# Pooled attention with a gated feed-forward block: order of the first loads and the copies of batch 0

## Chip, core and metric

One core of a Trainium2 chip. Times are device microseconds (us) of one execution. Its engines are TensorE (PE, with its weight loads as PEld), VectorE (DVE), ScalarE (ACT), GpSimd (POOL) and SyncE (SP); each works through its own queue in order.

## What is computed

q, k and v have 8 batches, 8 heads, 576 positions and 64 elements. k and v are averaged over groups of 8 positions, so that 72 keys and values remain; each of the 576 queries attends to these. The result goes, as 4608 tokens of 512 elements, through two matrices with a gate between them:

```
k_p = k.reshape(B, H, Sp, pool, D).mean(axis=3)
v_p = v.reshape(B, H, Sp, pool, D).mean(axis=3)
attn = softmax(scale * q @ k_p^T)
x = (attn @ v_p), heads side by side
h = x @ w_in
out = (h * cos(h)) @ w_out
```

## The kernel before

There are nine token tiles of 512 and eight batches of 576. The order of the work on each engine is the order in which it is written. Attention of batch 0 comes first, by itself; then, for each tile t, the up-projection (`up_mm`, L297, with cos on ScalarE L304 and the product on VectorE L307) and the down-projection (`down_mm`, L310), with the attention of the next batch filled in between the matmuls of the down-projection. Batches from 2 on are pooled by POOL (`pool_add`) and turned by DMA transposes; batches 0 and 1 are pooled and turned on TensorE.

**Layout of batches 0 and 1.** A tile of k, q or v has 128 partitions: the even head of a pair in partitions 0 to 63, the odd head in 64 to 127, nine positions in each partition, four pairs side by side. Pooling is a matmul with a matrix `groups` of ones and zeros, which VectorE builds from two iotas of POOL through `dist`, `sign` and `groups` (L361 to L365).

**PSUM.** `banks[0..2]` are three pairs of banks, `obanks[0]` and `obanks[1]` two single ones.

**The loads.** k's first two pairs come as fp32 by SP (L342) into a part of `g_sb` that is free then, and ScalarE casts them into the k tile (L343). All others are issued by POOL, with the cast in the transfer (L84): behind the three iotas (L347, L350) q's first two pairs, k's last two, q's last two, v, and then weights and batch 1.

**Batch 0, in the order written** (L397 to L420):
1. Ten warm-up matmuls; pooling of k's pairs 0 and 1 (`pool_k_mm`, 36 matmuls of 64x72, L157, even and odd heads in two halves of the partitions of obank1); four copies into `kk` by VectorE (`put_kk`, L132): each half is put on both halves of the partitions of `kk`.
2. Two warm-ups; nine transposes of q (`q_transpose_mm`, L192): blocks 0 to 4 into bank2, copied by VectorE, 5 to 8 into obank0, copied by ScalarE (L193). Two warm-ups.
3. Scores (L211) and exp (L218) of the first two units. A unit is 256 queries of four heads; `us[0]` and `us[1]` are heads 0 to 3, `us[2]` and `us[3]` are heads 4 to 7.
4. Pooling of k's pairs 2 and 3 into obank1, its four copies, the sums of `us[0]` (`sums_first`: matmuls with ones L266, then 1/sum on ScalarE as ln and exp, L270 and L271), transposes 9 to 17 of q into bank2 and obank0 and two copies, the sums of `us[1]` (obank1).
5. Scores and exp of `us[2]` and `us[3]` (`banks[0]` and `banks[2]`); pooling of v (`pool_v_mm`, L165, 18 matmuls 256 wide into the two banks of `banks[1]`) and one copy (L167); the sums of `us[2]` and `us[3]` and the values of all four (`values_then`: matmuls L280, product on VectorE L282 into `xT`).
6. The first quarter of the up-projection needs heads 0 to 3 alone (`up_mm(0, 0, 0, 2)`, `up_mm(0, 1, 0, 2)`), the rest all heads.

**Batch 1.** During tile 0, beside the up-projection (fp 4 to 6), k is pooled (pairs 0 and 1 into obank0, copied by VectorE, pairs 2 and 3 into obank1, copied by ScalarE) and q is transposed; v is pooled in the down-projection (L468).

Of the kernel before, what the change touches and what calls it, by code (L numbers as in the profile page):

```python
# [19 lines left out]
def kernel(  # L20
# [9 lines left out]
    nc = tc.nc  # L30
    B, H, S, D = q.shape
    Sp = S // POOL
# [4 lines left out]
    KCH = d_model // 128  # L37
# [9 lines left out]
    REST = (SEG[2], (0, H))  # L47
# [19 lines left out]
    kk = [wpool.tile([128, H, SpA], BF16, name=f"kk{i}") for i in range(2)]  # L67
# [4 lines left out]
    banks = [psum.tile([128, 2, 512], FP32, name=f"bank{i}") for i in range(3)]  # L72
# [5 lines left out]
    staged = {}  # L78
# [4 lines left out]
    def load_even(dst, b, src, j0=0, j1=KCH):  # L83
        nc.gpsimd.dma_start(out=dst[:, j0:j1].rearrange("p j t d -> p j (t d)"), in_=even_view(src, b, j0, j1))  # L84
# [38 lines left out]
    half = (slice(0, 64), slice(64, 128))  # L123

    def v_part(b):
        return vz[b % 2][:, :, 0:4:3, :]

    def put_kk(b, ps, pj0, pj1, copy):
        dst = kk[b % 2].rearrange("p (j a) n -> p j a n", a=2)
        for a in range(2):  # L130
            for r in range(2):
                copy(out=dst[half[r], pj0:pj1, a, 0:Sp], in_=ps[half[a]])  # L132

    def pool_add(b, which):

        st = staged.pop((which, b))
# [10 lines left out]
            s = s.rearrange("p (j a) t d -> p j a t d", a=2)  # L147
            add(out=v_part(b), in0=s[..., 0, :], in1=s[..., 1, :], op=ADD)

    def pool_k_mm(b, bank, pj0, pj1):  # L150

        kb = staged["k", b]
        ps = bank[:, 0:(pj1 - pj0) * Sp].rearrange("p (j n) -> p j n", n=Sp)
        for pj in range(pj0, pj1):
            for t in range(ROW):
                for rows in half:
                    nc.tensor.matmul(ps[rows, pj - pj0, :], lhsT=kb[rows, pj, t, :], rhs=groups[rows, t, :],  # L157
                                     start=(t == 0), stop=(t == ROW - 1))
        return lambda copy: put_kk(b, ps, pj0, pj1, copy)

    def pool_v_mm(b, pair):
        vb = staged["v", b]
        for t in range(ROW):
            for hp, rows in enumerate(half):
                nc.tensor.matmul(pair[:Sp, hp, 0:KCH * D], lhsT=groups[rows, t, :], rhs=vb[rows, :, t, :],  # L165
                                 start=(t == 0), stop=(t == ROW - 1))
        nc.vector.tensor_copy(out=v_part(b).rearrange("p j a d -> p a j d"),  # L167
                              in_=pair[:Sp, :, 0:KCH * D].rearrange("p a (j d) -> p a j d", j=KCH))

    def k_transpose(b):  # L170
        nc.sync.dma_start_transpose(out=kk[b % 2], in_=kp2[b % 2].rearrange("p h s d -> p (h s d)"))
# [14 lines left out]
    def q_transpose_mm(b, bank, g0, g1):  # L186

        if ("qT", b) not in att:
            qT_tile(b)
        ps = bank.bitcast(BF16)[:, 0:(g1 - g0) * 128].rearrange("p (g n) -> p g n", n=128)  # L190
        for g in range(g0, g1):
            nc.tensor.matmul(ps[:, g - g0, :], q_flat(b)[:, g * 128:(g + 1) * 128], identity, is_transpose=True)  # L192
        return lambda copy: copy(out=att["qT", b][:, g0:g1, :], in_=ps)  # L193
# [80 lines left out]
    def values_then(b, u, ao):  # L274

        (c0, n), (h0, nh) = u
        ex = att.pop(("ex", b, u))
        for i in range(nh):
            pj, hp = divmod(h0 + i, 2)
            nc.tensor.matmul(ao[hp * 64:hp * 64 + 64, (i // 2) * n:(i // 2 + 1) * n],  # L280
                             lhsT=vz[b % 2][:, pj, 3 * hp, :], rhs=ex[:, ex_col(u, i):ex_col(u, i) + n])
        nc.vector.tensor_mul(out=x_out(b, u, slice(0, 128)), in0=cols(ao, u), in1=cols(att.pop(("inv", b, u)), u))  # L282
# [58 lines left out]
    k_first = g_sb.rearrange("p f n -> p (f n)").bitcast(FP32)[:, 0:2 * ROW * D]  # L341
    nc.sync.dma_start(out=k_first.rearrange("p (j n) -> p j n", j=2), in_=even_view(k, 0, 0, 2))  # L342
    nc.scalar.copy(out=staged["k", 0][:, 0:2].rearrange("p j t d -> p (j t d)"), in_=k_first)  # L343

    row_of = consts.tile([128, ROW], FP32, name="row_of")
    for rows in half:
# [2 lines left out]
    first_of = consts.tile([128, Sp], FP32, name="first_of")  # L349
    nc.gpsimd.iota(first_of, pattern=[[POOL, Sp]], base=0, channel_multiplier=0,  # L350
                   allow_small_or_imprecise_dtypes=True)
    load_even(staged["q", 0], 0, q, 0, 2)
    load_even(staged["k", 0], 0, k, 2, 4)
    load_even(staged["q", 0], 0, q, 2, 4)
    load_even(staged["v", 0], 0, v)
# [33 lines left out]
    def warm_up(n, bank):  # L389

        for i in range(n):
            nc.tensor.matmul(bank, lhsT=warm[:, 0:128], rhs=warm)
# [2 lines left out]
    us = BY_HEADS  # L395

    warm_up(10, obanks[0])  # L397
    pool_k_mm(0, obanks[1], 0, 2)(vec)
    warm_up(2, banks[1][:, 0, :])
    puts = q_transpose_mm(0, banks[2][:, 0, :], 0, 5), q_transpose_mm(0, obanks[0], 5, 9)  # L400
    puts[0](vec)
    puts[1](act)
    warm_up(2, banks[1][:, 0, :])
    scores(0, us[0], banks[0])
    scores(0, us[1], banks[1])
    pool_k_mm(0, obanks[1], 2, 4)(vec)
    sums_first(0, us[0], banks[0][:, 0, :])
    for put in (q_transpose_mm(0, banks[2][:, 0, :], 9, 14), q_transpose_mm(0, obanks[0], 14, 18)):
        put(vec)
    sums_first(0, us[1], obanks[1])  # L410
    warm_up(2, banks[1][:, 0, :])
    scores(0, us[2], banks[0])
    scores(0, us[3], banks[2])
    pool_v_mm(0, banks[1])
    sums_first(0, us[2], obanks[0])
    values_then(0, us[0], obanks[1])
    values_then(0, us[1], banks[1][:, 0, :])
    sums_first(0, us[3], banks[2][:, 0, :])
    values_then(0, us[2], obanks[1])
    values_then(0, us[3], obanks[0])  # L420
# [4 lines left out]
    for t in range(NT):  # L425
        b = t + 1
        if t > 0:

            up_mm(t, 0, 0, 2)
            up_mm(t, 1, 0, 2)  # L430
        for fp in range(FFCH // 2):
            up_mm(t, fp, 2 if fp < 2 else 0)
            between = ()
            if t == 0:
                if fp == 4:
                    puts = pool_k_mm(1, obanks[0], 0, 2), pool_k_mm(1, obanks[1], 2, 4)
                elif fp in (5, 6):
                    g0 = 9 * (fp - 5)
                    puts = q_transpose_mm(1, obanks[0], g0, g0 + 5), q_transpose_mm(1, obanks[1], g0 + 5, g0 + 9)
                if fp in (4, 5, 6):  # L440
                    puts[0](vec)
                    between = ((puts[1], act),)
            up_g(t, fp, between)
            if 0 < t and b < B:
                if fp == 0:
                    q_transpose(b)
                elif fp == 2:
                    k_transpose(b)
        mms = [(ms, fc) for ms in range(4) for fc in range(FFCH)]
        if t == 0:  # L450
            mms = [(ms, fc) for hm in range(2) for cg in range(4) for ms in range(2 * hm, 2 * hm + 2)
                   for fc in range(4 * cg, 4 * cg + 4)]


        def S_(n, bank):
            return lambda: scores(b, us[n], banks[bank])

        later = []

        def V_(n, bank, wait=None):  # L460
            return lambda: values(b, us[n], banks[bank], wait)

        fill = []
        if t < B:
            exp_tables()
            fill = [(1, lambda: scores(t, REST, banks[2])), (16, lambda: values(t, REST, banks[1]))]
        if t == 0:
            fill[1:] = [(2, S_(0, 0)), (8, lambda: pool_v_mm(1, banks[1])), (8, lambda: values(t, REST, banks[2])),  # L468
                        (11, S_(1, 0)), (13, V_(0, 1)), (18, S_(2, 2)), (21, V_(1, 0, later)), (26, S_(3, 1)),
                        (32, lambda: later.pop()()), (32, V_(2, 2)), (40, V_(3, 0))]  # L470
        elif b < B:
            us = BY_TOKENS

            def scores_of(*parts):

                def go():
                    for f in scores_mm, scores_exp:
                        for b_, u, bank in parts:
                            f(b_, u, banks[bank])
                return go  # L480

            fill = [(4, scores_of((b, us[0], 2), (b, us[1], 0))), (14, V_(0, 1, later)), (16, lambda: later.pop()()),
                    (19, V_(1, 2)), (35, scores_of((b, us[2], 0), (b, us[3], 1), (t, REST, 2))),
                    (38, V_(2, 0)), (43, lambda: values(t, REST, banks[1])), (46, V_(3, 2))]
        fi = 0
        if t == NT - 1:
            mms = mms[:-FFCH]
        for n, (ms, fc) in enumerate(mms):
            while fi < len(fill) and fill[fi][0] <= n:
                fill[fi][1]()  # L490
                fi += 1
            down_mm(obanks[ms % 2], ms, fc)
            if fc == FFCH - 1:
                down_out(t, ms, obanks[ms % 2])
        if t < B:
            sin_tables()
        if 0 < t and b + 1 < B:

            nc.gpsimd.tensor_copy(out=gate, in_=kk[b % 2][0:1, 0, 0:1])  # L499
        if b + 1 < B:  # L500
            load_kv(b + 1, "k", k)
            load_q(b + 1)
            load_kv(b + 1, "v", v)
            pool_add(b + 1, "k")
            pool_add(b + 1, "v")
# [29 lines left out]
```

The softmax here doesn't subtract the row's maximum and nothing guards it: scores larger than these inputs give would overflow.

## Time and profile before

| what | us |
|---|---|
| median of four runs | 302.15 (301.62 to 302.44) |
| the profiled execution | 301.98 |
| its span | 300.2 |
| TensorE busy | 291.5 |
| ScalarE busy | 205.6 |
| VectorE busy | 171.0 |
| POOL busy | 130.5 |

By the chain that ended last, TensorE carries 91% of the span. Times of rows count from the start of the span. A row of the timeline has a start, the busy time, the engine, line, operation, what it writes and reads, its shape and number, and in brackets the idle time before it with what ended it. The granted clock of TensorE is given as 1.00 for the core. From about 4 us to 33 us the DMA engines carry 190 to 210 GB/s.

### The profile page before, as it was taken

To read this page: it belongs to the slowest core of one execution; us is meant where nothing else is said; L and a number is where in the kernel's file an instruction comes from. 1 tells how busy PE (TensorE), PEld (TensorE's weight loads), DVE (VectorE), ACT (ScalarE), POOL (GpSimd) and SP (SyncE) were. 2 spreads that over 40 slices of the span, in tenths; PEclk is the share of its full clock that TensorE was granted. 3 is DMA by queue.
4 is the path that set the end of the run, shared out by engine and by line. 5 is a ranking of instruction groups with operands and counts; after the bars stand their busy time and mean duration, and the time that the engine had idled before them with its cause. 6 is when DMAs were issued, how large, how long until landed. Compare 5 with 4: busy or idle time off the path is not lost.

```text
span 300.2 us, 4592 instructions
## 1 busy us (share of the span) xinstructions
PE 291.5 (97%) x1783; PEld 143.2 (48%) x1816; DVE 171.0 (57%) x212; ACT 205.6 (68%) x254; POOL 130.5 (43%) x93
## 2 busy tenths in 40 slices
PE   8899999999999999999999999999999999999995
PEld 3545544445544454445444544455445544444444
DVE  5558546574566546754675566654675477415712
ACT  3887896469866987688768886789568966605500
POOL 8463018975963497339813990399200000000000
PEclk9999999999999999999999999999999999999999
DMA  7999999739436942696079617791811120131023
GB/s 159 202 207 207 209 203 194 161 57 177 91 81 120 174 106 49 133 169 129 17 156 153 133 23 171 102 168 37 142 31 35 37 70 0 37 70 35 0 67 75
DMA packets 44165, 32.91 MB, mean 110 GB/s; under 512 B 22128, under 2 KB 39408, under 8 KB 44144
## 3 DMA queue, kind: packets, MB, share of 16 engines
q0 software_dynamic: 19744, 18.07, 38.3%
q1 hardware_dynamic: 24160, 14.42, 20.5%
q8 instruction: 14, 0.23, 0.3%
q10 hardware_dynamic: 240, 0.13, 0.2%
q14 instruction: 7, 0.06, 0.1%
HBM read 36.70 MB, written 9.44 MB: 154 GB/s over the span
## 4 chain that ended last, share of the span: by engine, by line
PE 91%; ACT 2%; issue 1%; DVE 0%
PE bank L297 41%; PE obank L310 40%; PE bank L241 5%; PE bank L211 3%; PE bank L328 1%; ACT ex L218 1%; PE obank L157 0%; ACT inv L271 0%; PE bank L165 0%; ACT lnc L270 0%; PE obank L192 0%; DVE xT L282 0%; DVE o_sb L316 0%
## 5 line engine op out<-in xcount | busy, mean ns | idle before, releaser
L310 PE MATMUL obank<-w_out_sb,g_sb 128*128 128x512 bf16 x542 | 129.0, 379 | 0.9 <-issue 0.2
L297 PE MATMUL bank<-xT,w_in_sb 128*128 128x512 bf16 x563 | 126.0, 379 | 0.8
L304 ACT ACTIVATE cos<-bank,half_pi 128x1024 f32<-128x1024 f32 x72 | 79.3, 1113 | 58.9 <-PE bank L297 57.7
L307 DVE TENSOR_TENSOR g_sb<-bank,cos 128x1024 bf16<-128x1024 f32 x72 | 87.4, 1224 | 42.5 <-ACT cos L304 42.4
L297 PEld LDWEIGHTS <-w_in_sb 128*128 128x128 bf16 x576 | 56.1, 98 | 67.9 <-issue 1.9
L310 PEld LDWEIGHTS <-g_sb 128*128 128x128 bf16 x560 | 52.7, 98 | 56.6 <-issue 2.0
L252 DVE TENSOR_TENSOR xT<-bank,inv 64x512 bf16<-64x512 f32 (+1 forms) x72 | 45.3, 629 | 40.8 <-ACT inv L248 40.1
L141 POOL TENSOR_TENSOR kv_st<-kv_st 72x2048 f32<-72x2048 bf16 x12 | 48.7, 4060 | 33.2 <-DMA kv_st<-in_k_dram 33.2
L247 ACT ACTIVATE lnc<-bank 64x512 f32<-64x512 f32 (+1 forms) x72 | 39.2, 544 | 3.1 <-PE bank L241 1.7
L316 DVE COPY o_sb<-obank 128x512 f32<-128x512 f32 x35 | 23.6, 690 | 30.9 <-PE obank L310 30.5
L218 ACT ACTIVATE ex<-bank 72x1024 bf16<-72x1024 f32 (+1 forms) x40 | 35.0, 929 | 8.5 <-PE bank L211 8.4
L142 POOL TENSOR_TENSOR kv_st<-kv_st 72x1024 f32<-72x1024 f32 x12 | 28.2, 2347 | 1.0
L248 ACT ACTIVATE inv<-lnc 128x512 f32<-128x512 f32 (+1 forms) x36 | 21.0, 583 | 1.1
L241 PE MATMUL bank<-ex,vz 72*128 72x256 bf16 (+1 forms) x176 | 20.0, 243 | 0.1
L241 PEld LDWEIGHTS <-vz 72*128 72x128 bf16 x176 | 13.6, 97 | 9.6 <-DVE xT L252 0.5
L145 POOL TENSOR_TENSOR kp<-kv_st 72x512 bf16<-72x512 f32 x12 | 14.9, 1265 | 0.5
L211 PE MATMUL bank<-qT,kk 64*72 64x256 bf16 (+1 forms) x192 | 12.9, 251 | 0.5 <-issue 0.3
L499 POOL COPY gate<-kk 1x1 bf16<-1x1 bf16 x5 | 0.9, 182 | 26.5 <-DMA kk<-kp 26.5
L211 PEld LDWEIGHTS <-kk 64*72 64x72 bf16 x192 | 7.5, 109 | 9.9 <-issue 7.2
L285 ACT ACT_TABLE_LOAD x9 | 11.5, 1283 | 0.9 <-PEq L519 0.7
L288 ACT ACT_TABLE_LOAD x9 | 11.5, 1283 | 0.2
L103 POOL DMA_DIRECT2D kv_st<-in_v_dram x6 | 5.1, 848 | 8.8 <-PE bank L165 8.8
(55 smaller groups left out, 93.3 us busy)
## 6 DMA issues: line engine op xcount, KB each, us to landing
out_dram<-o_sb SPq DMA_DIRECT2D x70, 128.0 KB, 2.4
kv_st<-in_v_dram POOLq DMA_DIRECT2D x8, 576.0 KB, 13.6
kv_st<-in_k_dram POOLq DMA_DIRECT2D x7, 576.0 KB, 7.5
q_b<-in_q_dram POOLq DMA_DIRECT2D x6, 576.0 KB, 9.7
w_in_sb<-in_moe_w_in_dram POOLq DMA_DIRECT2D x4, 512.0 KB, 13.2
w_out_sb<-in_moe_w_out_dram POOLq DMA_DIRECT2D x4, 512.0 KB, 18.5
q_b<-in_q_dram POOLq DMA_DIRECT2D x4, 288.0 KB, 11.9
g_sb<-in_k_dram SPq DMA_DIRECT2D x1, 576.0 KB, 3.7
```

Source lines behind the costliest of these rows:

```text
L141: add(out=s, in0=x[:, :, 0:4, :], in1=x[:, :, 4:8, :], op=ADD)
L142: add(out=s[:, :, 0:2, :], in0=s[:, :, 0:2, :], in1=s[:, :, 2:4, :], op=ADD)
L211: nc.tensor.matmul(pair[:Sp, bank, c:c + n].rearrange("p (g n) -> p g n", n=64), lhsT=kk[b % 2][half[r], h0 + i, 0:Sp], rhs=att["qT", b][h ...
L218: nc.scalar.activation(out=ex[:, 0:nh * n].rearrange("p (a n) -> p a n", a=2), in_=pair[:Sp, :, 0:nh * n // 2], func=ACTF.Exp, scale=scale ...
L241: nc.tensor.matmul(pair[:, hp, (i // 2) * n:(i // 2 + 1) * n], lhsT=vz[b % 2][:, pj, 2 * hp:2 * hp + 2, :].rearrange("p a d -> p (a d)"), ...
L247: nc.scalar.activation(out=lnc[half[1 - hp]], in_=pair[half[1 - hp], hp, 0:w], func=ACTF.Ln)
L252: nc.vector.tensor_mul(out=x_out(b, u, half[hp]), in0=cols(pair[half[hp], hp, :], u), in1=cols(inv[half[1 - hp]], u))
L297: nc.tensor.matmul(h[:, j, :], lhsT=w_in_sb[fc // 4][:, ki, (fc % 4) * 128:(fc % 4 + 1) * 128], rhs=xT[:, ki, t * TILE:(t + 1) * TILE], st ...
L304: nc.scalar.activation(out=cos, in_=h, func=ACTF.Sin, bias=half_pi[:, :1])
L307: nc.vector.tensor_mul(out=g_sb[:, 2 * fp:2 * fp + 2, :], in0=h, in1=cos)
L310: nc.tensor.matmul(o, lhsT=g_sb[:, fc, ms * 128:(ms + 1) * 128], rhs=w_out_sb[fc // 4][:, fc % 4, :], start=(fc == 0), stop=(fc == FFCH - 1))
L316: nc.vector.tensor_copy(out=o[:, 0:n], in_=ps)
```

## The change

Three things are changed, with the functions that serve them:
- POOL issues the load of q's first two pairs before the iotas.
- `pool_k_mm` gets a list of two banks: even heads go to the lower half of one, odd heads to the upper half of the other, and it returns two puts, one for each bank (two copies each). In batch 0 the first put of pairs 0 and 1 goes to ScalarE, the second to VectorE; for pairs 2 and 3 both go to VectorE. Batch 1 pools all four pairs at once into the two banks: two copies on VectorE, two on ScalarE, each twice as wide as before.
- `pool_v_mm` gets two banks and a range of pairs, with one copy for each bank. Batch 0 calls it twice: pairs 0 and 1 into obank0 and obank1, pairs 2 and 3 into the two banks of `banks[1]`. Batch 1 calls it once, with two copies.

With them some banks change: transposes 5 to 8 of q go to the second bank of `banks[1]`, transposes 14 to 17 to the second bank of `banks[2]`, the values of `us[1]` to `banks[0]`.

```
-    def pool_k_mm(b, bank, pj0, pj1):
+    def pool_k_mm(b, ps, pj0, pj1):
         kb = staged["k", b]
-        ps = bank[:, 0:(pj1 - pj0) * Sp].rearrange("p (j n) -> p j n", n=Sp)
+        ps = [p[half[a], 0:(pj1 - pj0) * Sp].rearrange("p (j n) -> p j n", n=Sp) for a, p in enumerate(ps)]
         for pj in range(pj0, pj1):
             for t in range(ROW):
-                for rows in half:
-                    nc.tensor.matmul(ps[rows, pj - pj0, :], lhsT=kb[rows, pj, t, :], rhs=groups[rows, t, :],
+                for a in range(2):
+                    nc.tensor.matmul(ps[a][:, pj - pj0, :], lhsT=kb[half[a], pj, t, :], rhs=groups[half[a], t, :],
                                      start=(t == 0), stop=(t == ROW - 1))
-        return lambda copy: put_kk(b, ps, pj0, pj1, copy)
+        dst = kk[b % 2].rearrange("p (j a) n -> p j a n", a=2)
+        def put(a):
+            def go(copy):
+                for r in range(2):
+                    copy(out=dst[half[r], pj0:pj1, a, 0:Sp], in_=ps[a])
+            return go
+        return put(0), put(1)

-    def pool_v_mm(b, pair):
+    def pool_v_mm(b, ps, pj0=0, pj1=KCH):
         vb = staged["v", b]
+        ps = [p[:Sp, 0:(pj1 - pj0) * D] for p in ps]
         for t in range(ROW):
             for hp, rows in enumerate(half):
-                nc.tensor.matmul(pair[:Sp, hp, 0:KCH * D], lhsT=groups[rows, t, :], rhs=vb[rows, :, t, :],
+                nc.tensor.matmul(ps[hp], lhsT=groups[rows, t, :], rhs=vb[rows, pj0:pj1, t, :],
                                  start=(t == 0), stop=(t == ROW - 1))
-        nc.vector.tensor_copy(out=v_part(b).rearrange("p j a d -> p a j d"),
-                              in_=pair[:Sp, :, 0:KCH * D].rearrange("p a (j d) -> p a j d", j=KCH))
+        for hp in range(2):
+            nc.vector.tensor_copy(out=v_part(b)[:, pj0:pj1, hp, :], in_=ps[hp].rearrange("p (j d) -> p j d", d=D))
...
     nc.scalar.copy(out=staged["k", 0][:, 0:2].rearrange("p j t d -> p (j t d)"), in_=k_first)
+    load_even(staged["q", 0], 0, q, 0, 2)
...
-    load_even(staged["q", 0], 0, q, 0, 2)
     load_even(staged["k", 0], 0, k, 2, 4)
...
     warm_up(10, obanks[0])
-    pool_k_mm(0, obanks[1], 0, 2)(vec)
+    puts = pool_k_mm(0, obanks, 0, 2)
+    puts[0](act)
+    puts[1](vec)
     warm_up(2, banks[1][:, 0, :])
-    puts = q_transpose_mm(0, banks[2][:, 0, :], 0, 5), q_transpose_mm(0, obanks[0], 5, 9)
+    puts = q_transpose_mm(0, banks[2][:, 0, :], 0, 5), q_transpose_mm(0, banks[1][:, 1, :], 5, 9)
     puts[0](vec)
     puts[1](act)
-    warm_up(2, banks[1][:, 0, :])
+    warm_up(2, banks[0][:, 0, :])
     scores(0, us[0], banks[0])
     scores(0, us[1], banks[1])
-    pool_k_mm(0, obanks[1], 2, 4)(vec)
+    for put in pool_k_mm(0, obanks, 2, 4):
+        put(vec)
     sums_first(0, us[0], banks[0][:, 0, :])
-    for put in (q_transpose_mm(0, banks[2][:, 0, :], 9, 14), q_transpose_mm(0, obanks[0], 14, 18)):
+    for put in [q_transpose_mm(0, banks[2][:, i, :], 9 + 5 * i, 14 + 4 * i) for i in range(2)]:
         put(vec)
...
-    pool_v_mm(0, banks[1])
+    pool_v_mm(0, obanks, 0, 2)
+    pool_v_mm(0, (banks[1][:, 0, :], banks[1][:, 1, :]), 2, 4)
     sums_first(0, us[2], obanks[0])
     values_then(0, us[0], obanks[1])
-    values_then(0, us[1], banks[1][:, 0, :])
+    values_then(0, us[1], banks[0][:, 0, :])
...
                 if fp == 4:
-                    puts = pool_k_mm(1, obanks[0], 0, 2), pool_k_mm(1, obanks[1], 2, 4)
+                    puts = pool_k_mm(1, obanks, 0, 4)
...
-            fill[1:] = [(2, S_(0, 0)), (8, lambda: pool_v_mm(1, banks[1])),
+            fill[1:] = [(2, S_(0, 0)), (8, lambda: pool_v_mm(1, [banks[1][:, i, :] for i in range(2)])),
```

## The prediction

> **What bounds the kernel now.** I read the page first (busy shares, chain that ended last), then the chain of waits over the first 34 us, then the timeline of the first 19 us engine by engine, then the busy time and DMA rate in slices of 0.4 us.
>
> ```profile
> PE 291.5 (97%) x1783; PEld 143.2 (48%) x1816; DVE 171.0 (57%) x212; ACT 205.6 (68%) x254; POOL 130.5 (43%) x93
> PE bank L297 41%; PE obank L310 40%; PE bank L241 5%; PE bank L211 3%; PE bank L328 1%; ACT ex L218 1%; PE obank L157 0%; ACT inv L271 0%; PE bank L165 0%; ACT lnc L270 0%; PE obank L192 0%; DVE xT L282 0%; DVE o_sb L316 0%
> ```
>
> TensorE is busy for 97%, and four fifths of the chain are the two big multiplications (L297, L310). They gain nothing here: the change lies in the start, batch 0, and in a few copies for batch 1 at 26 to 38 us. So what counts is when the up-projection can begin. The chain of waits (start, length, what), followed back from there:
>
> ```profile
> 14.76 0.91 ACT ex L218
> 15.67 0.49 ACT lnc L270
> 16.18 0.64 ACT inv L271
> 16.84 0.61 ACT lnc L270
> 17.47 0.64 ACT inv L271
> 18.14 0.70 DVE xT L282
> 18.88 7.10 PE bank L297 x32
> ```
>
> Until 18.1 the chain is ScalarE. Its timeline (start, length, then in brackets the idle time before and what ended it) shows how far back that reaches:
>
> ```profile
> 4.49 1.15 ACT L343 CAST kv_st<-g_sb 128x1152 bf16<-128x1152 f32 x1 [2.46 <-DMA g_sb<-in_k_dram]
> 8.40 0.59 ACT L193 COPY qT<-obank 128x512 bf16<-128x512 bf16 x1 [2.76 <-PE obank L192]
> 9.48 1.93 ACT L218 ACTIVATE ex<-bank 72x1024 bf16<-72x1024 f32 x2 [0.49 <-PE bank L211]
> ...
> 13.75 1.91 ACT L218 ACTIVATE ex<-bank 72x1024 bf16<-72x1024 f32 x2
> ```
>
> From 9.48 to 18.12 no row of ScalarE has idle time before it. What happens there on other engines costs nothing while it is in time for ScalarE; the start of the first exp, 9.48, moves the rest one for one. What leads to it:
>
> ```profile
> 5.85 1.29 PE L157 MATMUL obank<-groups,kv_st 64*64 64x72 bf16 x36
> 7.07 0.80 PE L392 MATMUL bank<-warm 128*128 128x512 bf16 x2
> 7.18 1.28 DVE L132 CAST kk<-obank 64x144 bf16<-64x144 f32 x4 [2.32 <-PE obank L157]
> 7.70 0.44 PE L192 MATMUL bank<-identity,q_b 128*128 128x128 bf16 x5
> 8.49 0.49 DVE L193 COPY qT<-bank 128x640 bf16<-128x640 bf16 x1
> 9.04 0.63 PE L211 MATMUL bank<-qT,kk 64*72 64x256 bf16 x8 [0.24 <-DVE qT L193]
> ```
>
> k's first half lands at 4.45 (issued by SP at 0.75, 3.7 to landing), is cast by ScalarE until 5.64, pooled on TensorE from 5.85 (the cast is 0.16 us early: the ten warm-ups end only at about 5.8). Then two branches meet at the scores: VectorE makes four kk copies and one qT copy, done at 8.98; TensorE goes on through warm-ups and transposes and ScalarE copies the other qT part from 8.40 to 8.99. **They end 0.01 us apart.**
>
> **Part 1, the kk copies of the first two pairs on two engines.** Two of four copies leave VectorE: 2 x 0.306 us (median of L132) plus gaps, about 0.65. Its kk copies end at about 7.82 instead of 8.46; its qT copy then waits for the fifth transpose (8.14) and runs 8.17 to 8.66, 0.32 earlier. ScalarE's two copies (0.274 each by its L132 rows in batch 1) fill 7.18 to 7.75 of the 2.76 us that it idles. But ScalarE's qT copy is tied to the transposes, which end at 8.37 on a TensorE that has had no gap since 5.85, so it still ends at 8.99. The scores go in the order of heads 0, 2, 1, 3; head 2 needs blocks 5 to 8, ScalarE's part. So head 0 may start at 8.75, head 2 stays at 9.04, and the exp waits for all four. Gain: 0.00 to 0.05, I take 0. New banks bring no wait here: nobody else uses them.
>
> **Part 2, q ahead of the iotas.** POOL's 0.88 us issue (1.43 to 2.31) goes in front of three iotas (0.85 to 1.44). Each costed:
> - The iotas, 0.88 later, delay VectorE's dist, sign, groups: groups is ready at about 4.6 instead of 3.71; needed at 5.85. Hidden by 1.2 us. The memsets after it end at about 5.75 instead of 4.86; VectorE is next needed at 7.18. Without that cover it would be the full 0.88. POOL's queue behind (k's second half, q's, v, identity, weights) has the same work ahead of it: 0 to 0.1 us.
> - q lands 0.68 us earlier (issue at 0.75 as SP's and ScalarE's first instructions, instead of 1.43): 6.05 for 6.73 (5.3 to landing). The transposes load it at 7.47. Worth nothing.
> - The transfer meets k's first half, which is on the path. The slices (DMA share, GB/s last):
>
> ```profile
> 2.40:2.80 0.40, 0.40 (x3) 0.12 (x2) 0.40 (x1) 0.00 (x0) 0.40 (x1) 1.00 1.01 380
> 2.80:3.20 0.40, 0.40 (x3) 0.12 (x2) 0.37 (x1) 0.00 (x0) 0.40 (x2) 1.00 1.02 380
> 3.20:3.60 0.40, 0.40 (x3) 0.12 (x2) 0.39 (x1) 0.00 (x0) 0.40 (x1) 1.00 1.01 305
> 3.60:4.00 0.40, 0.40 (x2) 0.13 (x1) 0.24 (x2) 0.00 (x0) 0.40 (x2) 1.00 0.76 130
> ```
>
> At 380 GB/s k is alone; the rate bends in the third slice, about 3.4, 2.0 us after q's issue began: q has joined when k is nearly through. By the sums of the slices 510 of k's 590 KB are over by 3.4; with the join at 2.75 only 265 are. The Trainium skill, page "DMA: Bandwidth & Descriptors", section "Queues, rings and completion order", says that every DMA engine takes turns between the queues that have work, packet by packet, whichever engine issued them. That speaks against this change. By the row alone (a queue at 380 GB/s that the later one leaves untouched) the cost is 0; by the rule 325 KB at half of 380 take 1.72 us instead of 0.86, ending at 4.47 where before 80 KB took 0.42 and ended at 3.82: landing +0.65. The 305 and 130 of the last two slices, with the DMA still 0.76 to 1.01 busy, look like sharing, so I take the rule. Ends: 0, and +1.2 (q joins at 2.0 or so, since VectorE, which was at work on dist and sign while q was being issued, now waits for the iotas, and k shares nearly all its way). A gain is excluded: an earlier q cannot shorten the overlap.
>
> +0.65 at the landing is about +0.5 at the pooling (0.16 of slack). Then TensorE's clock: the warm-ups run 0.43 us apart up to 4.86, and the pair at 7.07 still 0.40, while full-speed L297 matmuls take 0.22. The rise comes at about 7.4, though the PEclk column reads 1.00 throughout. If it stays there, the pair of warm-ups and the end of the pooling, now behind it, run at twice the speed and give back 0.1 to 0.2. Transposes, ScalarE's copy and the exp: +0.3 to +0.5, taken +0.4.
>
> **Part 3, the rest of batch 0.** Second half of k: four copies on VectorE as before, same order; the second group of transposes goes to the other half of bank2 instead of obank0, and scores us[3], which overwrites bank2, needed both qT copies already. 0. v in two halves: TensorE issues 36 matmuls of half the width for 18 (by columns equal to L165's 1.15 us; up to 0.2 more, by L157's 36 in 0.77). New wait: the first half's odd matmul goes to obank1, which ScalarE's ln of us[1] reads until 13.19, while v's matmuls began at 13.07; behind it in TensorE's queue is the rest of v, then the sums of us[2]. VectorE: four copies at about 0.29 (0.306 for 144 columns, 0.69 for 512) for one of 0.69, in two steps, done at 15.05 or so instead of 15.00. The sums of us[2] wait for the exp that ends at 14.75 anyway: cover 0.3 us. Also banks[0] in place of banks[1] for the values of us[1]: the up-projection's first group waits for that VectorE product in any case, for its input. 0; without cover 0.1 to 0.3.
>
> **Part 4, batch 1** (the rewritten helpers): pooled keys are copied after all 72 matmuls (27.27) instead of after the first 36, but in two copies of 288 columns, about 0.46 each on VectorE and 0.40 on ScalarE, instead of four. VectorE ends at 28.2 for 27.99, ScalarE at 28.1 for 28.44; the product L307 behind goes 0.2 later, its result is needed from 33 on. v's copy, 0.69, becomes two of 0.43, until 38.2; next on bank1 is L241 at 38.9. TensorE is 15.8 of 16 us busy between 17 and 33. 0.
>
> **Sum**: the profiled execution took 301.98 (span 300.2, 1.8 around it), the median of the runs is 302.15. 0 + 0.4 + 0 + 0: 302.4 on the profiled execution, 302.55 on the median.
>
> **Rivals**, with 0.2% (0.6 us, about what a measurement of this kernel tells from no change) as the bound:
> - q shares nearly all of k's transfer. Place: k's landing; price: +1.2 there, +1.0 at the pooling, less 0.15 from the clock: 303.0. It decides once k lands after about 5.25. For: VectorE is idle while q is issued. Against: before, q's traffic came up slowly (130 GB/s in its first slice). Chance 0.27. Slower.
> - The clock. TensorE would now idle 0.5 us or more between warm-ups and pooling. The skill, page "TensorE: Matmul & The Clock Gate", section "Part 1: The HAM clock gate", lets full speed come only after a busy window of some 3.4 us, free-running. The row has the rise 5.9 us after the first matmul, later than that rule's shortest; if the gap spoils the window, pair, transposes and scores stay at half speed, +0.6 on top of +0.4: 303.2. Chance 0.15. Slower.
> - No sharing, k lands as before: 302.1. For: the packets of the later queue start slowly. Chance 0.15.
> - Faster: the transposes wait for q in most executions and the profiled one was lucky; then the earlier q and the split copies together give up to 0.7: 301.5. Against: this execution lies only 0.17 below the median, and q is 0.7 us early in it. Chance 0.13.
>
> The forecast itself has 0.30, mostly within 0.2%. Same: 0.30 + 0.15 = 0.45; slower 0.27 + 0.15 = 0.42; faster 0.13. The range, 301.9 to 303.3, takes in the bounds 0 and +1.2 and leaves out the faster case and a little above.
>
> **What would show it.** Right: landing of k's first half near 5.1, its cast ending near 6.3, pooling near 6.35, ScalarE's qT copy ending near 9.4 with VectorE's done earlier, first exp near 9.9, ScalarE without idle from there to its table load, the up-projection's stretch later by as much. Wrong: k landing at 4.45; transposes that wait for q; idle time of ScalarE behind the first exp, or TensorE waiting at 13 to 15 us for obank1 or the v copies.

## The result, and the profile after

The changed kernel takes 302.67 us (median of 31 executions) against 302.21 for the kernel before (51 on the same chips). The medians are 0.46 us apart; the ratio, 1.002 with a 95% interval of 1.0012 to 1.0028, stands for 0.36 to 0.85 us. Two of the 31 executions (307.43 and 305.75), and four of the twelve with three more iotas below, ran at a lower granted clock (0.976 to 0.989); only those above 307 are left out of the ratios. The changed kernel is slower: none of its executions is below 302.45, of the kernel before 39 of 51 are. The median lies within the stated range, 0.12 above the stated time. **But the time is lost 30 us behind the place where the prediction put it.**

The profiled execution took 302.89, its span is 301.1. It is 0.2 slower than the median, so that the two profiles lie 0.9 apart and not 0.46. First ScalarE's timeline of the changed kernel (start, length, idle before):

```profile
4.24 1.15 ACT L348 CAST kv_st<-g_sb 128x1152 bf16<-128x1152 f32 x1 [2.21 <-DMA g_sb<-in_k_dram]
6.58 0.57 ACT L159 CAST kk<-obank 64x144 bf16<-64x144 f32 x2 [1.18 <-PE obank L152]
8.06 0.59 ACT L198 COPY qT<-bank 128x512 bf16<-128x512 bf16 x1 [0.91 <-PE bank L197]
9.11 1.93 ACT L223 ACTIVATE ex<-bank 72x1024 bf16<-72x1024 f32 x2 [0.46 <-PE bank L216]
...
17.75 1.28 ACT L293 ACT_TABLE_LOAD   x1
```

k's first half is cast from 4.24, not later than before (4.49): nothing slowed its transfer. The first exp starts at 9.11 instead of 9.48 and the stretch ends at 17.75 instead of 18.12. Batch 0 is *shorter* in this execution. Now TensorE's timeline of the changed kernel: pooling of k, transposes, the first matmul of v's pooling, the start of the down-projection, the first matmuls that need the second quarter of w_out, and the next tile's up-projection:

```profile
5.77 0.77 PE L152 MATMUL obank<-groups,kv_st 64*64 64x72 bf16 x36
...
7.35 0.68 PE L197 MATMUL bank<-identity,q_b 128*128 128x128 bf16 x9 [0.26 <-DMA q_b<-in_q_dram]
...
13.35 0.69 PE L170 MATMUL obank<-kv_st,groups 64*72 64x128 bf16 x18 [0.43 <-DMA kv_st<-in_v_dram]
...
33.02 0.38 PE L315 MATMUL obank<-w_out_sb,g_sb 128*128 128x512 bf16 x1
...
38.29 0.81 PE L315 MATMUL obank<-w_out_sb,g_sb 128*128 128x512 bf16 x3 [1.13 <-DMA w_out_sb<-in_moe_w_out_dram]
...
53.69 6.45 PE L302 MATMUL bank<-xT,w_in_sb 128*128 128x512 bf16 x29
```

The last three in the kernel before:

```profile
33.40 0.38 PE L310 MATMUL obank<-w_out_sb,g_sb 128*128 128x512 bf16 x1
...
37.37 0.81 PE L310 MATMUL obank<-w_out_sb,g_sb 128*128 128x512 bf16 x3
...
52.77 7.53 PE L297 MATMUL bank<-xT,w_in_sb 128*128 128x512 bf16 x33
```

Three brackets name a DMA that no row of TensorE waited for before: q, v, and, for 1.13 us, w_out. The balance: the down-projection begins 0.38 ahead, the matmuls on w_out's second quarter and everything behind them are 0.92 behind. That is the 0.9 by which the spans differ: 1.30 lost at this one place, less the 0.38 gained before it.

Why does w_out land late? POOL's timeline, first of the kernel before, then of the changed kernel:

```profile
0.85 0.32 POOL L347 IOTA row_of<- 64x9 f32 x2 [0.39 <-POOLq L519]
1.24 0.20 POOL L350 IOTA first_of<- 128x72 f32 x1
1.43 0.88 POOL L84 DMA_DIRECT2D q_b<-in_q_dram  x1
2.30 0.74 POOL L84 DMA_DIRECT2D kv_st<-in_k_dram  x1
...
5.16 2.25 POOL L112 DMA_DIRECT2D w_in_sb<-in_moe_w_in_dram  x3
...
19.35 0.75 POOL L117 DMA_DIRECT2D w_out_sb<-in_moe_w_out_dram  x1
```

```profile
1.26 0.87 POOL L84 DMA_DIRECT2D q_b<-in_q_dram  x1 [0.81 <-POOLq L528]
2.22 0.35 POOL L353 IOTA row_of<- 64x9 f32 x2
2.64 0.20 POOL L356 IOTA first_of<- 128x72 f32 x1
2.78 0.76 POOL L84 DMA_DIRECT2D kv_st<-in_k_dram  x1
...
5.81 2.25 POOL L112 DMA_DIRECT2D w_in_sb<-in_moe_w_in_dram  x3
...
19.86 0.75 POOL L117 DMA_DIRECT2D w_out_sb<-in_moe_w_out_dram  x1
```

q goes at 1.26, only 0.17 earlier than before, and not at 0.75: the bracket says that POOL's own sequencer was not ready. Most of the iotas used to run inside that time, from 0.85 to 1.44; now they follow, and everything behind them is late: k's second half by 0.48, the first weights by 0.65, w_out's second quarter by 0.51.

By the trace's packets (bytes as written, after the cast) POOL's loads had moved 604 KB by 7.5 us before and 520 after. From about 10 us to 42 us they flow at an even 200 to 207 GB/s in both kernels, so that the shortfall stays: 81 to 82 KB at 10, 20, 30 and 40 us, worth 0.40 us at 206 GB/s. w_out's second quarter landed at 37.13 before, 0.24 ahead of its first matmul; it now lands at 38.25, 1.12 later. The shortfall explains 0.40 of that. The rest is in the order of the packets: when this load landed, 6795 KB of the stream had moved instead of 6660, so 135 KB more (some 0.65 us) of the loads issued *behind* it had gone ahead of its last packet. Why that share differs between executions is open (table below).

One caution for reading two profiles: the 36 pooling matmuls took 1.29 us before and take 0.77 here, because TensorE doubled its speed earlier. The warm-up matmuls show when: they follow each other every 0.43 us, and every 0.22 from some point on. Over the executions profiled below that point lies anywhere between 4.5 and 7.4 us, with the granted clock shown as 1.00 throughout. Much of the 0.37 by which batch 0 is ahead is likely that, not the change.

### The profile page after: what moved, and what is told of

Read it like the earlier page. It is cut to its first block, busy times and chain, and to the rows that moved or that the text cites. A ratio compares the mean times of both kernels' runs of the same rounds, so it can differ in the third digit from the quotient of the medians.

```text
span 301.1 us, 4629 instructions
## 1 busy us (share of the span) xinstructions
PE 291.4 (97%) x1801; PEld 142.9 (47%) x1834; DVE 170.6 (57%) x212; ACT 206.0 (68%) x254; POOL 130.7 (43%) x93
## 4 chain that ended last, share of the span: by engine, by line
PE 85%; DMA 10%; POOL 3%; issue 1%; ACT 1%; DVE 0%; POOLq 0%
PE obank L315 39%; PE bank L302 37%; DMA w_out_sb<-in_moe_w_out_dram 6%; PE bank L246 5%; DMA w_in_sb<-in_moe_w_in_dram 3%; PE bank L216 3%; PE bank L333 1%; POOL kv_st L84 1%; ACT ex L223 1%; POOL kp L390 1%; POOL q_b L84 1%; POOL vz L388 0%; POOL identity masks.py:197 0%; POOL row_of L353 0%; DVE o_sb L321 0%
## 5 line engine op out<-in xcount | busy, mean ns | idle before, releaser
L84 POOL DMA_DIRECT2D q_b<-in_q_dram x10 | 7.7, 770 | 3.4 <-DMA w_in_sb<-in_moe_w_in_dram 1.9
```

## The experiments

Each was timed against the kernel before on the same chip; the ratio is given with its 95% interval. Theories: **late stream** (POOL's loads are late and TensorE runs into them), **copies and banks** (the new banks, halves and copies cost), and the prediction's own, **q shares k's transfer**.

**One part alone: q ahead.** `load_even(staged["q", 0], 0, q, 0, 2)` moved ahead of the iotas in the kernel before.

> The kernel before with q's first load ahead of the iotas and nothing else changed. Late stream (POOL's later loads go some 0.5 us later and the second quarter of w_out, which TensorE needs at about 37.3 us, lands near 38.2 instead of 37.15): w_out's second quarter waited for, slower than before by 0.5 to 1.0 us, 302.7 to 303.2. Copies and banks to blame: as before, 302.2. q shares k's transfer, as predicted: k's first half lands near 5.1 and the first exp starts 0.4 later than 9.48.

302.45 against 302.00, ratio 1.0018 (1.0011 to 1.0024): the load alone brings the whole loss. k's cast starts at 4.23, so q does not share its transfer. The same landings are late (q 7.51, v 13.38, w_out's second quarter 37.75). TensorE meets v first:

```profile
13.43 1.17 PE L165 MATMUL bank<-kv_st,groups 64*72 64x256 bf16 x18 [0.28 <-DMA kv_st<-in_v_dram]
14.72 0.41 PE L266 MATMUL obank<-ex,ones 72*64 72x256 bf16 x4
15.43 0.41 PE L280 MATMUL obank<-ex,vz 72*64 72x256 bf16 x4 [0.30 <-DVE vz L167]
...
16.70 0.63 PE L280 MATMUL obank<-ex,vz 72*64 72x256 bf16 x8 [0.42 <-DVE xT L282]
...
37.27 0.41 PE L241 MATMUL bank<-ex,vz 72*128 72x64 bf16 x8
...
37.80 0.81 PE L310 MATMUL obank<-w_out_sb,g_sb 128*128 128x512 bf16 x3
```

A late v makes the undivided pooling and copy of v late, and the values behind it. But of that only 0.14 is left when the down-projection begins (33.54 for 33.40). The larger part is lost at w_out again: its matmuls start at 37.80, 0.05 after the landing and 0.43 later than before. The row has no bracket, since matmuls' ends are modelled and the idle time that is left, 0.12, is too short to be shown.

**The other parts alone: copies, banks and halves.** The changed kernel with q's load back behind the iotas.

> The changed kernel with q's load back behind the iotas, so the copies, banks and halves alone. Late stream: w_out's second quarter lands at 37.2 again, no wait of 1.1 us before the down-projection, 301.9 to 302.2. Copies and banks to blame: as the changed kernel, 302.7.

302.24 against 302.00, ratio 1.0010 (1.0002 to 1.0017): a little slower where as fast or faster was expected. TensorE waits 0.48 for w_out's second quarter, which lands at 37.58. TensorE is early there (the down-projection begins at 33.00, 0.40 ahead of the kernel before), and the stream, which had moved as much by 5 us as before, falls 62 KB behind by 15 us without a change in POOL's first issues (1.42, 2.30, 3.03, 3.84). So the start of the stream varies by itself, and neither expectation holds fully.

**POOL's queue alone.** Three more iotas between q's load and k's second half in the kernel before; their result isn't read.

```
     load_even(staged["q", 0], 0, q, 0, 2)
+    nc.gpsimd.iota(spare_row[rows], ...)      # both halves
+    nc.gpsimd.iota(spare_first, ...)
     load_even(staged["k", 0], 0, k, 2, 4)
```

> The kernel before with three more iotas of the same shapes on POOL between q's first load and k's second, written to tiles that nobody reads; VectorE's work stays early, as before. Late stream through POOL's queue alone: k's second half is issued near 2.9, the software queue is some 80 KB behind by 7.5 us, w_out's second quarter lands near 38, 302.6 to 302.9. VectorE's later work on dist, sign and groups beside POOL's issues to blame: no shortfall in the slices of 4.4 to 5.6 us, as before, 302.2.

303.40 against 302.00, ratio 1.0059 (1.0032 to 1.0086); the eight executions below 306 have a median of 303.1. More than expected: 0.56 us of iotas on POOL, whose result nobody waits for, cost about 1 us. k's second half is issued at 2.87 and lands at 9.70 (8.46 before); TensorE waits for k, q, v (0.66) and w_out's third quarter (0.54). The stream is 99 KB behind by 7.5 us and 199 KB from 15 us on, almost 1 us of it. Why it falls back by more than the delay is not shown: POOL's own waits for landings (0.65 us for k) delay later issues, but at that time some 3 MB were issued and not yet moved. A later queue alone is enough to make the kernel slower.

**The wait taken away by other data.** The changed kernel; the first two row groups of tile 0 read w_out's first quarter for the second, so that this part of the result is left out.

```
+        cg = 0 if early and fc // 4 == 1 else fc // 4
```

> The changed kernel with the wait taken away by other data: for the first two row groups of tile 0 the down-projection reads w_out's first quarter where it should read the second, so that part of the result is left out. Late stream: no wait at 37 us, 0.5 to 1.0 us faster than the changed kernel, 301.7 to 302.2, unless the third quarter (lands near 40.5) is late next. Copies and banks to blame: 302.7, the time is lost elsewhere.

302.35 against 302.00, ratio 1.0014 (1.0005 to 1.0023). The second quarter is not waited for; the third is late next, at 40.59. Its timeline:

```profile
39.32 0.59 PE L316 MATMUL obank<-w_out_sb,g_sb 128*128 128x512 bf16 x2
40.64 0.59 PE L316 MATMUL obank<-w_out_sb,g_sb 128*128 128x512 bf16 x2 [0.73 <-DMA w_out_sb<-in_moe_w_out_dram]
```

The whole stream is late, not one load. The changed kernel with no later quarter waited for was not run.

**No later quarter waited for, with and without the copies.** Both kernels have q behind the iotas and read w_out's first quarter in place of all four in those row groups (`cg = 0 if early else fc // 4`).

> The kernel before; for the first two row groups of tile 0 the down-projection reads w_out's first quarter in place of all four, so that part of the result is left out and no landing of the later quarters is waited for. If the stream of loads just keeps pace in the kernel before (second quarter lands at 37.15, wanted at about 37.2): as before, 301.9 to 302.0. If it already holds TensorE up in most executions: faster by 0.2 or more.

> The copies, banks and halves alone (q behind the iotas), with the same edit of the down-projection, which leaves the same part of the result out. If the copies make batch 0 shorter by 0.2 to 0.4 and the late stream hides it: faster than the same edit on the kernel before by 0.2 to 0.4, 301.6. If the copies are worth nothing, as predicted (ScalarE's qT copy is tied to the transposes): equal to it, 302.0.

301.97 (ratio to the kernel before 0.9992, 0.9983 to 1.0002) and 301.63 (0.9982, 0.9972 to 0.9991). The two intervals overlap; set against each other directly, the 13 and the 9 executions have means of 302.00 and 301.58, 0.42 apart (0.18 to 0.66 by resampling them). So with w_out's landing out of the way the copies, banks and halves together gain. The timelines show where; first without them, in an execution where TensorE doubled its speed at 4.6:

```profile
12.95 1.17 PE L165 MATMUL bank<-kv_st,groups 64*72 64x256 bf16 x18 [0.68 <-DMA kv_st<-in_v_dram]
14.05 0.41 PE L266 MATMUL obank<-ex,ones 72*64 72x256 bf16 x4
14.96 0.41 PE L280 MATMUL obank<-ex,vz 72*64 72x256 bf16 x4 [0.49 <-DVE vz L167]
...
16.82 8.82 PE L297 MATMUL bank<-xT,w_in_sb 128*128 128x512 bf16 x40
```

and with them:

```profile
13.08 0.70 PE L170 MATMUL bank<-kv_st,groups 64*72 64x128 bf16 x18
14.09 0.41 PE L271 MATMUL obank<-ex,ones 72*64 72x256 bf16 x4 [0.31 <-ACT ex L223]
14.31 0.41 PE L285 MATMUL obank<-ex,vz 72*64 72x256 bf16 x4
```

With v in one piece its copy holds the values up for 0.49; in halves nothing waits for it. v landed 0.37 earlier in the second (12.54 for 12.91), so these two do not settle what the halves are worth. A third execution does, that of the kernel with w_out ahead below, whose batch 0 is the same as in the second: its speed doubled at 4.5, its first exp starts at 8.56 (8.52 in the first), v lands at 12.90.

```profile
12.94 0.69 PE L170 MATMUL obank<-kv_st,groups 64*72 64x128 bf16 x18 [0.57 <-DMA kv_st<-in_v_dram]
...
14.31 0.38 PE L285 MATMUL obank<-ex,vz 72*64 72x256 bf16 x4
...
16.08 8.97 PE L302 MATMUL bank<-xT,w_in_sb 128*128 128x512 bf16 x40
```

At the same landing of v the up-projection begins at 16.08 instead of 16.82, and 0.59 are left of that when the down-projection begins (32.47 for 33.06).

**k's second half ahead of the iotas too.**

> The kernel before with q's first load and k's second half ahead of the iotas (alone, no copies changed). q goes at 1.26, k at 2.13, iotas at 3.0 to 3.6, the later loads as late as with q alone ahead (w_in near 5.8); groups is ready near 5.9, pooling is hardly late. If the shortfall is the gap between the first two loads (the DMA engines have too little queued at 4 to 6 us): second quarter of w_out near 37.2, 302.0. If it is that all later loads are issued 0.5 us later: near 37.7, as with q alone ahead, 302.4.

302.71 against 302.19, ratio 1.0015 (1.0006 to 1.0024), as with q alone ahead: closing the gap between the first two loads (1.27 and 2.13) does not help. The later ones are late (q's second 3.51, w_in 5.55), and w_out's second quarter lands at 37.72.

**VectorE's work beside POOL's issues.** dist, sign and a spare copy of groups computed once more, 3.6 to 5.9 us.

> The kernel before with VectorE's dist, sign and a copy of groups computed a second time (into a tile that nobody reads) behind groups, so that VectorE is at work beside POOL's issues from 3.7 to 6 us, as it is in the changed kernel; POOL's queue is as before. If VectorE's work there is what slows the start of the software queue: some 90 to 130 KB moved by 5 us instead of 150, q's first load lands at 7.2 or later instead of 6.7, the later loads 0.3 to 0.5 later, 302.3 to 302.5. If POOL's queue alone does it: q at 6.7, second quarter of w_out at 37.1, 302.0.

302.58 against 302.17, ratio 1.0012 (1.0003 to 1.0022). The slow start is there as expected (103 KB by 5 us, q at 7.20), and so is the late landing (w_out's second quarter at 38.22). But the link between them is not: by 10 us the stream had moved as much as before, and it is 10 KB behind at 30 us. At that landing 200 KB more had moved than before, so that the delay is nearly all one of order among the loads. The iotas' move sends the same VectorE work to about the same time in the changed kernel.

**Less work of VectorE there.** The copies alone, with the memset of vz moved behind the first qT copy.

> The copies alone (q behind the iotas), with VectorE's 0.91 us memset of vz moved from 3.9 us, where the software queue starts, to behind the first qT copy, where VectorE is idle. If that memset slows the queue's start as dist and sign do: more than 160 KB moved by 5 us, second quarter of w_out at 36.9 to 37.1, and with the halves of v faster than the kernel before by 0.2 to 0.4. If not: as the copies alone, 302.0 to 302.3.

302.54 against 302.24, ratio 1.0009 (0.9997 to 1.0021). Not faster; and in its profiled execution the stream started slowest of all (71 KB by 5 us, q at 8.75) with VectorE idle from 3.8 to 7.0. So VectorE's work cannot be the only thing that slows the start.

**w_out's second quarter ahead of v** (batch 1), with v pooled five matmuls later, in the kernel with the copies alone.

> The copies alone, with w_out's second quarter loaded ahead of batch 1's v, and v pooled five matmuls later in the down-projection. If the stream holds back the gain of the copies: second quarter lands near 35, v near 37.7 with its pooling at about 39, no wait until the third quarter (near 40), 301.7 to 301.9. If the copies are worth nothing: 302.0 to 302.2.

303.23 against 302.19, ratio 1.0036 (1.0024 to 1.0048): slower, by six executions. w_out landed at 34.20 as wanted, but v only at 37.41, and the attention of batch 1, packed tighter, waits for ScalarE and VectorE instead.

**q by SP.** q's first two pairs loaded as fp32 into the free part of g_sb, behind k, and cast by VectorE; with the copies, and without.

```
+    nc.sync.dma_start(out=q_first.rearrange("p (j n) -> p j n", j=2), in_=even_view(q, 0, 0, 2))
+    nc.vector.tensor_copy(out=staged["q", 0][:, 0:2].rearrange("p j t d -> p (j t d)"), in_=q_first)
```

> The copies alone, with q's first two pairs loaded as fp32 by SP behind k's first half into the free part of g_sb and cast by VectorE, so that POOL's queue has one load less. If the stream of POOL's loads holds back the copies: k's second half is issued near 1.4 instead of 2.3, w_out's second quarter lands near 36.5, no wait there, faster than the kernel before by 0.3 to 0.7, 301.3 to 301.7. If it does not: 302.0 to 302.3.

> The kernel before with the same load of q by SP and the cast on VectorE, no copies changed. If the stream only just keeps pace in the kernel before, an earlier stream alone gives little: 301.7 to 302.0, and less than together with the copies.

302.32 (1.0002, 0.9994 to 1.0010) and 302.18 (0.9997, 0.9989 to 1.0005): as the kernel before. POOL issues k's second half at 1.43, as expected, yet by the trace's packets not a byte of it moves until 5.24. The slices of the first of the two (from and to, busy time of TensorE, its weight loads, VectorE, ScalarE and POOL, granted clock, DMA share, GB/s):

```profile
3.60:4.00 0.40, 0.40 (x2) 0.13 (x1) 0.24 (x2) 0.00 (x0) 0.40 (x2) 1.00 1.04 403
4.00:4.40 0.40, 0.40 (x2) 0.15 (x1) 0.40 (x1) 0.00 (x0) 0.33 (x3) 1.00 1.05 415
4.40:4.80 0.40, 0.40 (x2) 0.15 (x1) 0.40 (x3) 0.34 (x1) 0.40 (x2) 1.00 1.03 409
4.80:5.20 0.40, 0.40 (x2) 0.15 (x1) 0.06 (x2) 0.40 (x1) 0.40 (x1) 1.00 0.98 386
5.20:5.60 0.40, 0.40 (x2) 0.00 (x0) 0.00 (x0) 0.40 (x1) 0.40 (x2) 1.00 1.23 225
```

SP's two loads have the DMA engines to themselves at some 400 GB/s until 5.2; only then do POOL's begin. The longer wait takes most of the early issue away: with q's 295 KB off its queue, POOL's stream is only 28 and 86 KB ahead, and w_out's second quarter still lands later than before. This also bears on why an earlier q did not disturb k: in all kernels with one load by SP POOL's first packets move at 3.4 to 3.8, when SP's last go (3.7 to 4.0), whether q was issued at 1.26 or at 1.43.

**All at one place.** TensorE's matmuls on w_out's second quarter come 3.97 us behind the start of the down-projection in the kernel before. What they come later than that is the time held:

| kernel | down-projection begins | quarter lands | its matmuls start | held | stream behind at 30 us, KB | more of later loads gone first, KB |
|---|---|---|---|---|---|---|
| before | 33.40 | 37.13 | 37.37 | - | - | - |
| changed | 33.02 | 38.25 | 38.29 | 1.30 | 82 | 135 |
| q ahead alone | 33.54 | 37.75 | 37.80 | 0.29 | 106 | 20 |
| q and k ahead | 33.53 | 37.72 | 37.76 | 0.26 | 91 | 29 |
| copies alone | 33.00 | 37.58 | 37.62 | 0.65 | 62 | 16 |
| VectorE's work twice | 33.41 | 38.22 | 38.26 | 0.88 | 10 | 200 |
| q by SP, copies | 33.18 | 37.60 | 37.64 | 0.49 | -28 | 109 |
| q by SP | 33.20 | 37.34 | 37.38 | 0.21 | -86 | 125 |

In all but the first TensorE starts 0.04 or 0.05 after the landing, and from these matmuls to the end of the span it is 262.8 to 263.1 us in every row. So in these executions it is the landing that sets the time, whatever batch 0 has gained; the last two columns, both against the kernel before, say what delays it (q's 295 KB by SP counted as moved).

No version here is faster than the kernel before with its whole computation.

## Why the prediction was right in size and wrong in cause

That the time came out as forecast is luck: the step that carried the +0.4 did not happen, and a cost that was put at 0 to 0.1 took its place. Two of the prediction's own signs of being wrong are in the profile: k is not late, and the transposes wait for q.

- **"The transfer meets k's first half"** failed; it carried the whole forecast of +0.4. It stood on 510 KB being over when the rate bends at 3.4, read as "2.0 us after q's issue began", and on an issue 0.68 earlier; the issue moved by 0.17. POOL's first packet moved at 3.48, for 3.43 before. k's cast began at 4.23 to 4.34 in four kernels with q ahead, within the 4.20 to 4.49 of those with q behind. The rule of turns taken packet by packet (the Trainium skill, page "DMA: Bandwidth & Descriptors", section "Queues, rings and completion order") could not be seen at work: from POOL's first packet to SP's last, 69 KB of SP's and 8 of POOL's moved in the changed kernel. Whether POOL's queue had packets ready before that and was passed over, or had none, no run shows.
- **"POOL's queue behind has the same work ahead of it: 0 to 0.1 us"** failed, and this is where the true cost begins: 0.48 to 0.65. The sum of the work is the same, but most of the iotas had run in a time in which POOL's first load could not be issued anyway (0.81 us of sequencer, row at 1.26). The prediction let that load start at 0.75 by analogy with SP and ScalarE, which was not measured for POOL.
- **"groups is ready at about 4.6"**: it is ready at 5.35, since the iotas start 1.37 later and not 0.88. It was needed at 5.77, so that of a cover put at 1.2 us 0.4 were left.
- **"q lands 0.68 us earlier: worth nothing"**: it lands later, 7.30 to 7.67 in four kernels with q ahead, against 6.53 to 6.75 in four with it behind and the rest of the front unchanged (7.28 and 8.75 in two more). TensorE waits 0.26 for it in the changed kernel.
- **Loads later in the queue were not costed at all**, although it is there that the kernel is tight: w_out's second quarter landed 0.24 us ahead of TensorE. A page that shows no wait for a DMA doesn't show how near one is; the landings beside the first use do.
- **Part 1, kk copies on two engines: 0 to 0.05.** Right in mechanism: head 0's scores start at 8.38, ScalarE's qT copy ends at 8.65, and the exp starts 0.46 behind it; with VectorE's copies in one piece it was 0.54 behind (q ahead alone). About 0.08, and up to 0.2 where VectorE's branch is the later one (0.68 behind with the spare iotas).
- **Part 3, halves of v: 0, without cover 0.1 to 0.3.** The cover was gone in executions where TensorE was fast early: there, at the same landing of v, the halves are worth 0.59. The gain is then hidden by w_out.
- **Part 4, batch 1: 0.** As predicted: its copies take 0.91 us on VectorE and 0.80 on ScalarE, for 1.26 and 1.13 before, and nobody waits for them.
- **The clock rival** could not be tested apart: no gap in front of the pooling arose (L152 at 5.77).

**What stays open:** why the stream of POOL's loads starts slower with q ahead (82 to 131 KB behind the kernel before at 20 us in four executions; with q behind between 25 ahead and 58 behind in five of six, 128 behind in the sixth). POOL's order alone (three iotas more) and VectorE's work alone (done twice) each make the kernel slower; the run with VectorE idle and a slow start fits neither. How the 0.46 divides between the two is not known, nor what decides how much of later loads goes ahead of w_out's last packet (up to 200 KB more than before), nor why the copies alone came out 0.1% slower. Each profile is one execution.

## What to carry to other kernels

Moving a load to the front of a queue moves everything else behind it: list the landings of *all* later loads beside their first use before calling the move free, for a stream that runs at its full rate doesn't make up a delay (here 81 to 82 KB from 10 us to 40). Work in front of a queue's first DMA can be all but free because that DMA isn't ready to go; taking it out of there puts its time on the queue. A gain ahead of a landing that sets the time doesn't show, and an early TensorE only waits longer. And a forecast that comes out right may still rest on a cause that isn't there: look for each step in the trace, not at the total.

## What the runs showed of the hardware

- POOL's first load begins no earlier than 1.26 us even with nothing ahead of it (four kernels, 1.26 to 1.27); SP's goes at 0.75.
- POOL's first packets moved only as SP's loads ran out: at 3.4 to 3.8 with one load of 590 KB by SP, whose last packets went at 3.7 to 4.0; at 5.1 and 5.2 with two, whose last went at 5.5 and 5.6.
- Loads in POOL's queue overlap: when v's last packet had ended (1152 bytes each), 71 to 309 packets of the weights issued behind it (1024 bytes each) had ended too, and the landing followed 0.3 to 0.4 us after that packet, in twelve executions.
- TensorE doubled its speed between 4.5 and 7.4 us after the start of the span in executions that all began their matmuls at 1.47; 36 small matmuls took 1.29 or 0.77 us accordingly, and the granted clock column read 1.00 for both.
